# First token's middle row: folded and split once for all batches, kept in DRAM, and put into each transform by DMA

## The chip, the cores and the metric

The kernel runs on one core of a Trainium2 chip. The core has five engines that work side by side and wait for one another through semaphores: TensorE (PE, with its weight loads as PEld), VectorE (DVE), ScalarE (ACT), GpSimd (POOL) and SyncE (SP), which here only issues DMAs. The metric is the device time of one execution in microseconds (us).

## The reference

Inputs are q, k, v of 4 batches, 8 heads, 768 tokens and 64 elements, and two weights. A window attention with four sink tokens gives x, and a Fourier mix with a feed-forward part follows:

```
B, H, S, D = q.shape                                   # 4, 8, 768, 64
scores = scale * matmul(q, k.transpose(0, 1, 3, 2))
keep = is_sink | in_window                             # 4 first keys, or the last 128
a = exp(scores - max); a = a / (sum(a) + 1e-09)
x = matmul(a, v)                                       # then to (B, S, H * D = 512)

X = fft(fft(x, axis=1), axis=2)                        # along tokens, then along the 512 columns
u = x + real(X)
un = (u - mean(u)) / sqrt(var(u) + 1e-06)
out = u + maximum(un @ w_ch1, 0.0) @ w_ch2
```

## The kernel before

**Stages.** The attention runs over 24 query blocks of 128 tokens (6 for each batch), each in four steps of one pair of heads, so 96 steps in all. Then the feed-forward part runs over six groups of four blocks; it takes the rest of the time and is not touched.

**The transform of one batch** is done inside the attention of the next batch, by the function `fourier`. Token n and token 768 - n enter the cosine sum with the same factor and the sine sum with opposite ones, and so do columns m and 512 - m. So the six blocks of a batch are first folded to three: `fold_n` adds and subtracts blocks j and 3 + j (one 128x512 operation on VectorE, one on GpSimd), `fold_m` folds the columns (128x255), `fold_hi` on ScalarE rounds the result to the short float that TensorE takes at speed (`gh`), and `fold_lo` on VectorE keeps the remainder (`gl`). Then come `stage1` (products with the constant matrices, into the banks `za`, `zr`, `zb`) and `stage2a`/`stage2b`, and `combine` and `update` add the real part to `u`.

**The first token** fits no pair: block 3 has a place for it in its row 0, but while the fold runs that place holds token 384 in another role. So the outputs of the first token are worked out apart for all batches at once, in steps 10 to 20 (`first_products` to `first_row`), and kept in DRAM (`x0_dram`, 32 rows of 64). Each transform reads its 512 numbers back (`load_row`, 33 equal copies, into the tile `xr`) and does four small operations with them:

- `put_row` (L379): copies the row into row 0 of block 3 of `u`, once the fold has read that block.
- `mid_sum` (L368): folds its columns, 33x255.
- `mid_hi` (L371): rounds the folded row into rows 0 to 32 of the tile `sph`, 33x257.
- `mid_row` (L376): replaces row 32 of `sph` by the remainder, 1x257.

Rows 0 and 32 of `sph` are what `stage1` uses: its last product into `za` and `zr` takes `sph` and adds the first token. The other rows of `sph` meet zeros. [...] All four operations are on VectorE, but for `mid_hi` of the last batch, which is on ScalarE.

**The order.** Up to step 97 the order of each engine is written out by hand: `at(step, engine, function)` puts a function into a step, and the table `SCHEDULE` says where in the step the events ("A", 0 to 3, "V", "G", "T") stand among the attention's own operations. An event "S" is issued by SyncE at the head of its step, behind the loads of q, k and v that belong there. After step 97 a scheduler sets the order; the fold and transform of the last batch fall into that part, together with the start of the feed-forward part and with the conversion of its weights (`convert`, L600 to L602, tiles `raw`, `cv`, `w2r`, three VectorE operations for each 512 columns).

**Buffers that set the pace.** A pair's scores `s` have two PSUM buffers: TensorE can write the scores of a pair when VectorE has read those of the pair before last (`merge` L727, `soft1` L739 with `sm` and `mx`). A block of v (`ldv`) has four buffers. SyncE issues its DMAs strictly in order, so a DMA that waits holds all behind it.

Of the kernel before, what the change touches and what calls it, by code (L numbers as in the profile page):

```python
# [11 lines left out]
F32 = mybir.dt.float32  # L12
F32R = mybir.dt.float32r
# [3 lines left out]
ALU = mybir.AluOpType  # L17
# [3 lines left out]
B, H, S, D = 4, 8, 768, 64  # L21
DM, DFF = H * D, 2048
# [3 lines left out]
NHALF = NB // 2  # L26
# [8 lines left out]
NR = 33  # L35
# [26 lines left out]
FILL_AT, FILL = (24, 36), 0  # L62
FOLD_AT, FOLD_LAST, FOLD_ENG = (0, 4, 8), (0, 4, 8), "VG"

F_N, F_M, F_S, ROW = (3, 3), (4, 5), (6, 7), (5, 8, 10)
EV_A = 0

SINK0_AT = 3, 3, "V"
# [143 lines left out]
def kernel(  # L212
# [14 lines left out]
    nc = tc.nc  # L227
    V, A, G, T = nc.vector, nc.scalar, nc.gpsimd, nc.tensor

    def f32(ap):  # L230
        return ap.bitcast(F32)
# [3 lines left out]
    dpool = ctx.enter_context(tc.tile_pool(name="dpool", bufs=1, space=bass.MemoryType.DRAM))  # L235
# [3 lines left out]

    w_dram = [dpool.tile([P, 2, len(LEFT) * 2 * P], F32, name=f"w2s{q}") for q in range(NF // 2)]  # L240
    x0_dram = dpool.tile([B * H, D], F32, name="x0d")


    prm = cpool.tile([P, 2, 2], I32, name="prm")
# [22 lines left out]
    def run(general):  # L267
        tag = "g" if general else ""
        with ExitStack() as p1:
# [5 lines left out]
            fw = pf.enter_context(tc.tile_pool(name="fw" + tag, bufs=1))  # L275
            ev = {}

            def at(s, eng, fn):
                ev.setdefault((s, eng), []).append(fn)
# [26 lines left out]
            sph = fpool.tile([P, 384], F32R, name="sph")  # L306
# [3 lines left out]
            def uview(b):  # L310
                if b not in us:
                    us[b] = ([U[b][:, j] for j in range(NB)] if b in U else
                             [fw.tile([P, DM], F32, tag=f"us{j}", name=f"us_{b}_{j}") for j in range(NB)])
                return us[b]
# [5 lines left out]
            def bank(b, name):  # L320
# [5 lines left out]
                pool, t, n = banks[turn[0] % len(banks)]  # L326
                return pool.tile([P, 512], F32, tag=t, name=f"{name}_{b}", bufs=n)

            def fourier(b, at, ready):
                u = uview(b)  # L330
                gh = npool.tile([P, NHALF, DM], F32R, tag="gh", name=f"gh_{b}", bufs=1)
# [3 lines left out]
                t_ = {}  # L335
# [3 lines left out]
                    return t_[name]  # L339

                def load_row():
                    t_["x0"] = fw.tile([NR, DM], F32, tag="xr", name=f"xr_{b}")
                    nc.sync.dma_start(t_["x0"], x0_dram[H * b:H * b + H].rearrange("(o h) d -> o (h d)", o=1).broadcast_to([NR, DM]))

                def fold_n(eng, j, odd):
                    t = fw.tile([P, DM], F32, tag=f"f{odd}", name=f"f{odd}_{b}_{j}", bufs=2 - odd)
# [16 lines left out]
                def fold_lo(j):  # L363
                    V.tensor_tensor(gl[:, j], t_.pop(("g", j)), f32(gh[:, j]), op=ALU.subtract)  # L364

                def mid_sum():
                    r = t_["x0"]
                    V.tensor_tensor(r[:, 1:256], r[:, 1:256], r[:, 511:256:-1], op=ALU.add)  # L368

                def mid_hi():  # L370
                    (A.copy if b == B - 1 else V.tensor_copy)(sph[:NR, :257], t_["x0"][:, :257])  # L371

                def mid_row():
                    t = t_["x0"]
                    lo = sph[NR - 1:NR, :257]
                    V.tensor_tensor(lo, t[NR - 1:NR, :257], f32(lo), op=ALU.subtract)  # L376

                def put_row():
                    V.tensor_copy(u[NHALF][0:1], t_["x0"][0:1])  # L379

                def stage1(kind, mc, part, parts):
                    ps = t_[f"z{kind}{mc}"] if part else psum(f"z{kind}{mc}")
# [77 lines left out]
                        nc.sync.dma_start(u_dram[b][:, blk, :], t)  # L460

                tail = b == B - 1 or general
                at(1, "S", load_row)
                for j in range(NHALF):
                    k = ready[j]
                    e0, e1 = FOLD_TAIL if tail else FOLD_ENG
# [4 lines left out]
                    at(k + F_M[1], e1, lambda j=j: fold_m(eng[e1], j, 1))  # L471
                    at(k + F_S[0], "A", lambda j=j: fold_hi(j))
                    at(k + F_S[1], "V", lambda j=j: fold_lo(j))
                at(ready[0] + ROW[0], "V", put_row)
                at(ready[0] + ROW[1], "V", mid_sum)
                at(ready[0] + ROW[2], "A" if b == B - 1 else "V", mid_hi)
                at(ready[0] + ROW[2], "V", mid_row)
                k = ready[2] + S1
                n1, na, nb = PARTS_TAIL if tail else PARTS[b]
                for i, (kind, mc) in enumerate((("a", 0), ("a", 1), ("r", 0), ("b", 0), ("b", 1))):  # L480
                    n = n1[i]
# [10 lines left out]
                for i, j in enumerate(FFT_ORDER):  # L492
# [9 lines left out]
                    for r in range(2):  # L502
                        e = UPD_TAIL[r] if b >= B - 2 else "G"
                        n = 2 * i + r
# [147 lines left out]
            hp = []  # L652

            def window_attention(fourier, load_constants):
                with ExitStack() as pa:
                    kpool = pa.enter_context(tc.tile_pool(name="kpool", bufs=1, side="right"))
# [187 lines left out]
                    with ExitStack() as man:  # L844
# [6 lines left out]
                        def take(n, rows=P, dtype=F32):  # L851
                            took[0] += n
                            t = scratch[:rows, took[0] - n:took[0]]
                            return t if dtype == F32 else t.bitcast(dtype)
# [66 lines left out]
                        x0 = take(D, B * H)  # L921
# [19 lines left out]
                        def first_row(i):  # L941
                            if i == 0:
                                V.tensor_scalar(fs[:, 0], fs[:, 0], fm[:, 2:3], None, op0=ALU.mult)
                                V.tensor_scalar(x0, fin[:, 1 + NS], fs[:, 0, 0:1], None, op0=ALU.mult)
                            else:
                                V.scalar_tensor_tensor(x0, fin[:, 1 + NS + i], fs[:, 0, i:i + 1], x0, op0=ALU.mult, op1=ALU.add)
                            if i == NS - 1:
                                nc.sync.dma_start(x0_dram, x0)
# [12 lines left out]
                        at(15, "A", first_exp)  # L961
                        for i in range(NS):
                            at(17 + i, "V", lambda i=i: first_row(i))

                        table = {
                            "merge": merge, "soft1": soft1, "expo": expo, "sink_p": sink_p, "trans_p": trans_p, "copy_p": copy_p,
# [4 lines left out]
                        s = 0  # L971
                        extra.append(lambda name: ps_t.tile([P, 512], F32, tag="x", name=name)
                                     if s % NP in X_AT and not X_NOT[0] <= s <= X_NOT[1] and s < len(steps) - 2 else None)
                        while s < last:
# [21 lines left out]
                            if s == 0:  # L996
                                a, b, e = SINK0_AT
                                at(a, "A", lambda: sink_hi(0))
                                at(b, e, lambda: sink_lo(0))
                            for e in "AVGT":  # L1000
                                for op in SCHEDULE[s >= PHASE][e][k]:
                                    if op in EVENTS:
                                        if (s, op) == (4, "G"):
                                            load_constants()
                                        run_ev(s, op)
                                    elif op in STEP_LAG:
                                        lag(table[op], s, STEP_LAG[op])
                                    else:
                                        at_ = s - BLOCK_AT[op]
                                        if at_ % NP == 0 and 0 <= at_ // NP < NQ:  # L1010
                                            table[op](at_ // NP)
                                            if op == "store_x" and at_ // NP % NB == 3:
                                                b = at_ // NP // NB
                                                fourier(b, lambda d, e, f, s=s: at(s + d, e, f), FOLD_AT if b < B - 1 else FOLD_LAST)
                            s += 1
                    extra.clear()
                return last

            def general_attention(fourier):
                for b in range(B):  # L1020
                    u = uview(b)
                    with ExitStack() as pa:
# [19 lines left out]
                        for j, blk in enumerate(Q_BLOCKS):  # L1042
# [22 lines left out]
                            for h in range(H):  # L1065
                                r = slice(D * (h % 2), D * (h % 2) + D)
# [24 lines left out]
                        x0 = gw.tile([1, DM], F32, tag="gq", name=f"gx0_{b}")  # L1091
                        V.tensor_copy(x0, u[NHALF][0:1])
                        V.tensor_copy(u[NHALF][0:1], u[0][0:1])
                        nc.sync.dma_start(x0_dram[H * b:H * b + H].rearrange("(o h) d -> o (h d)", o=1), x0)
                    ev = []
                    fourier(b, lambda d, e, f: ev.append((d, ENGINES.index(e), len(ev), f)), FOLD_AT)
                    for it in sorted(ev, key=lambda t: t[:3]):
                        it[3]()

            if general:  # L1100
                load_constants()
                general_attention(fourier)
                normalize(0, 8, 22, lambda i: None)
                start_ffn(40)
                s = 0
                while ev:
                    for e in ENGINES:
                        run_ev(s, e)
                    s += 1
            else:  # L1110
                s = window_attention(fourier, load_constants)
# [322 lines left out]
            with tc.manual_schedule():  # L1434
# [3 lines left out]
                for g in range(1, len(groups)):  # L1438
# [70 lines left out]
                    for _ in steps:  # L1509
                        pass  # L1510

    run(False)
    with tc.tile_pool(name="tpool2", bufs=1) as tp:
        t0 = tp.tile([P, 2], F32, name="t1")
# [8 lines left out]
    with tc.If(general != 0):  # L1523
        run(True)
# [77 lines left out]
```

## Time and profile before

| | |
|---|---|
| median of 3 runs | 768.49 us (767.43 to 771.24) |
| the profiled execution's own time | 768.74 us |
| its span | 767.0 us |
| TensorE busy | 742.3 us (97%) |
| VectorE busy | 600.6 us (78%) |
| ScalarE busy | 345.9 us (45%) |
| GpSimd busy | 181.6 us (24%) |

How to read the rows in this document. A row of a timeline has start, duration, engine, line, operation, output and inputs, and in brackets how long the engine had been idle and what released it. A row of the chain of waits has start, duration on the chain, engine, output tile and line; the chain is followed back from the last instruction, at each step to what released it. A row of the windows has the stretch in us, then busy time (and instructions) of TensorE, its weight loads, VectorE, ScalarE and GpSimd, then the granted TensorE clock (1.00 is full), the share of the DMA engines and GB/s. Matmul ends are modelled.

The attention and the four transforms take the first 283 us of the span. The folds of the four batches stand at about 48 to 72 us, 100 to 130 us, 158 to 190 us and 215 to 235 us.

### The profile page before, as it was taken

The numbers are of one execution on the slowest core, as the hardware profiler recorded it, in microseconds if no ns is written. First come the engines' busy times: TensorE is split into PE (matmuls) and PEld (weight loads), VectorE is DVE, ScalarE is ACT, GpSimd is POOL, SyncE is SP. The second block draws the span as 40 slices with busy tenths as digits, with TensorE's granted clock in tenths as the row PEclk, the third lists the DMA queues.
The fourth block names the chain that finished last, engine by engine and source line by source line (L and its number), as shares of the span: only waits on it lengthen the run. The fifth ranks groups of instructions, "written<-read, shape, count | busy, mean of one in ns | idle before, by whom it ended". The sixth has DMA issues, their size and how long they took to land.

```text
span 767.0 us, 14157 instructions
## 1 busy us (share of the span) xinstructions
PE 742.3 (97%) x4903; PEld 626.7 (82%) x4903; DVE 600.6 (78%) x1641; ACT 345.9 (45%) x896; POOL 181.6 (24%) x286
## 2 busy tenths in 40 slices
PE   7999998998999999999999999999999999999996
PEld 5666775766788778788989899899899998998995
DVE  6878588799799989969877978778895888764435
ACT  4877666666643223444545333333333333333330
POOL 2557267467574445400000000000000000000001
PEclk9999999999999999999999999999999999999998
DMA  9845514532313446323546757755577557556661
GB/s 294 277 112 165 144 56 151 160 104 94 111 56 138 138 165 219 110 110 141 190 151 247 227 160 231 230 171 191 170 226 235 173 172 243 160 176 188 208 193 60
DMA packets 95008, 129.40 MB, mean 169 GB/s; under 512 B 5932, under 2 KB 60844, under 8 KB 94544
## 3 DMA queue, kind: packets, MB, share of 16 engines
q1 hardware_dynamic: 94352, 124.26, 51.1%
q0 software_dynamic: 288, 3.76, 1.3%
q8 instruction: 41, 0.67, 0.4%
q10 hardware_dynamic: 288, 0.39, 0.1%
q14 instruction: 39, 0.32, 0.1%
HBM read 104.26 MB, written 24.13 MB: 167 GB/s over the span
## 4 chain that ended last, share of the span: by engine, by line
PE 78%; DVE 16%; issue 2%; ACT 1%; POOL 1%; DMA 1%; SPq 0%; DVEq 0%; ACTq 0%; POOLq 0%
PE h L638 31%; PE p L1313 25%; PE xt L808 5%; PE s L721 5%; PE o L1139 3%; PE pt L770 2%; PE za L393 2%; PE zb L393 1%; DVE f L348 1%; PE x L820 1%; DVE sm L739 1%; DVE gl L364 1%; PE zr L393 1%; DVE w2r L602 1%; DMA vt<-in_v_sink_dram 1%
## 5 line engine op out<-in xcount | busy, mean ns | idle before, releaser
L1313 PE MATMUL p<-w_ring,h_sums 128*128 128x256 f32 x936 | 131.3, 283 | 0.1
L1313 PEld LDWEIGHTS p<-w_ring,h_sums 128*128 128x128 f32 x936 | 122.9, 191 | 3.6 <-DVE u L1143 0.3
L1261 ACT CAST h_sums<-sums 128x256 fp32r<-128x256 f32 (+2 forms) x158 | 89.7, 568 | 70.5 <-PE p L1313 28.6
L1262 DVE TENSOR_TENSOR h_sums<-sums,h_sums 128x256 fp32r<-128x256 f32 (+2 forms) x158 | 98.3, 622 | 17.5 <-ACT h_sums L1261 16.5
L1313 PE MATMUL p<-w2t,h_sums 128*128 128x256 f32 x702 | 110.3, 283 | 0.0
L1335 POOL TENSOR_TENSOR u<-u,u 128x512 f32<-128x512 f32 x3 | 3.8, 1293 | 422.9 <-DVE u L1335 422.9
L1313 PEld LDWEIGHTS p<-w2t,h_sums 128*128 128x128 f32 x702 | 97.9, 191 | 3.1
L638 PE MATMUL h<-un_slots,w 128*128 128x512 f32 x396 | 96.5, 392 | 0.0
L638 PE MATMUL h<-un_last,w 128*128 128x512 f32 x396 | 96.4, 392 | 0.0
L638 PEld LDWEIGHTS h<-un_slots,w 128*128 128x128 f32 x396 | 72.7, 188 | 14.0
L638 PEld LDWEIGHTS h<-un_last,w 128*128 128x128 f32 x396 | 72.3, 188 | 14.4 <-DVE un_slots L553 0.7
L745 ACT ACTIVATE sm<-sm,mx 128x132 f32<-128x132 f32 x192 | 75.8, 399 | 14.4 <-DVE mx L739 14.4
L1475 ACT ACTIVATE sums<-h 128x512 f32<-128x512 f32 x40 | 23.9, 597 | 96.8 <-PE h L638 96.8
L721 PE MATMUL s<-ring,q 64*128 64x260 f32 x320 | 55.6, 430 | 7.2 <-DVE mx L739 7.2
L1163 DVE STREAM_TRANSPOSE unf<-un 32x128 f32<-32x128 f32 x192 | 58.1, 302 | 2.8
L1272 DVE TENSOR_TENSOR sums<-sums 128x256 f32<-128x256 f32 x39 | 16.4, 422 | 47.6 <-ACT sums L1475 47.3
L1443 ACT ACTIVATE sums<-h 128x512 f32<-128x512 f32 x40 | 23.9, 599 | 64.8 <-PE h L638 64.8
L739 DVE CUSTOM_DVE_ANT_0 sm<-s,mask 128x132 f32<-128x132 f32 x192 | 47.5, 285 | 4.5 <-PE s L719 2.4
L727 DVE COPY_PREDICATED s<-older,s 128x256 f32<-128x256 uint8 x80 | 33.8, 422 | 16.9 <-PE s L721 16.6
L721 PEld LDWEIGHTS s<-ring,q 64*128 64x128 f32 x320 | 25.0, 186 | 21.3 <-issue 10.0
L808 PE MATMUL xt<-ptl,ldv 128*64 128x128 f32 x384 | 39.8, 288 | 0.0
L745 ACT ACTIVATION_READ_ACCUMULATOR sm<-sm,mx 128x1 f32 x192 | 36.7, 191 | 0.0
(239 smaller groups left out, 1378.1 us busy)
## 6 DMA issues: line engine op xcount, KB each, us to landing
w_ring<-w2s SPq DMA_DIRECT2D x62, 512.0 KB, 4.3
w2t<-w2s SPq DMA_DIRECT2D x93, 256.0 KB, 3.2
raw<-in_moe_w_ch_dram SPq DMA_DIRECT2D x32, 512.0 KB, 3.3
w2s<-w_ring SPq DMA_DIRECT2D x16, 512.0 KB, 3.0
ldv<-in_v_dram SPq DMA_DIRECT2D x28, 256.0 KB, 2.8
ring<-in_qk_dram SPq DMA_DIRECT2D x24, 264.0 KB, 4.3
w2s<-w2t SPq DMA_DIRECT2D x24, 256.0 KB, 3.1
out_dram<-u SPq DMA_DIRECT2D x22, 256.0 KB, 4.6
```

What stands on the lines that cost most here:

```text
L393: T.matmul(ps[:, :NK], a, c, start=i == 0, stop=i == len(mm) - 1)
L638: T.matmul(ps[:, :tb], a[:, cs], x[:, :, cc, :], start=n == 0, stop=n == 3 * NCC - 1)
L721: T.matmul(ps[:, j, :P + W], st["q", g][rows, hp, :], keys(g, 2 * hp + j), start=True, stop=True)
L727: V.copy_predicated(ps[:, :, P + NS:P + W], older[qi > 2], ps[:, :, 0:P])
L739: V.tensor_tensor_reduce(sm[:, h % 4], ps[:, j, P:P + W], mask[min(qi, 3)], -SCALE, 3.0e38, ALU.add, ALU.min, accum_out=mx[:, 0, h:h + 1])
L745: A.activation(sm[:, h % 4], sm[:, h % 4], AF.Exp, bias=mx[:, 0, h:h + 1], scale=-1.0, accum_out=mx[:, 1, h:h + 1])
L808: T.matmul(ps[D * j:D * j + D, p, :], st["v", kb(g) - i][:, h, :], a[:, h % 4, :], start=i == 0, stop=i == n - 1)
L1163: V.transpose(unf[32 * q:32 * q + 32, :, r], un[r].rearrange("p (c q j) -> p c q j", c=NCC, q=4)[:, :, q])
L1261: A.copy(hc_hi[:, left(a, n)], src)
L1262: V.tensor_tensor(hc_lo[:, left(a, n)], src, f32(hc_hi[:, left(a, n)]), op=ALU.subtract)
L1313: T.matmul(acc[i][:, 2 * P * tp:2 * P * tp + 2 * P], x, w, start=q == 0 and tp == 0 and n == 0, stop=q == end and n == 2, skip_group_check ...
L1443: A.activation(r4[:, 0].rearrange("p t w -> p (t w)"), ps, AF.Relu)
```

## The change

The four operations on the row leave the transforms. A new function `middle_rows` does the fold and the split once for all four batches, in four partitions (one per batch), in steps 24 to 29 of the attention, and stores both halves in DRAM (`xm_dram`, per batch two rows of 257). Each transform then issues two DMAs on SyncE: `load_row` brings the two half rows straight into rows 0 and 32 of `sph`, nine steps after the start of `fourier`, and `put_row` brings the 512 numbers from `x0_dram` straight into row 0 of block 3, five steps after it.

```diff
-F_N, F_M, F_S, ROW = (3, 3), (4, 5), (6, 7), (5, 8, 10)
+F_N, F_M, F_S, ROW = (3, 3), (4, 5), (6, 7), (9, 5)
+ROW_AT = 24, 26, 27, 28, 29
...
+    xm_dram = dpool.tile([B, 2, DM // 2 + 1], F32, name="xmd")
...
+            def middle_rows(b, n, at):
+
+                x = fw.tile([B, DM], F32, tag="xr", name=f"xr_{b}")
+                xm = fw.tile([B, 2, DM // 2 + 1], F32R, tag="xm", name=f"xm_{b}")
+
+                def load():
+                    nc.sync.dma_start(x[:n], x0_dram[H * b:H * (b + n)].rearrange("(o h) d -> o (h d)", o=n))
+
+                def fold():
+                    V.tensor_tensor(x[:n, 1:256], x[:n, 1:256], x[:n, 511:256:-1], op=ALU.add)
+
+                def hi():
+                    A.copy(xm[:n, 0], x[:n, :257])
+
+                def lo():
+                    V.tensor_tensor(xm[:n, 1], x[:n, :257], f32(xm[:n, 0]), op=ALU.subtract)
+
+                def store():
+                    nc.sync.dma_start(xm_dram[b:b + n], f32(xm[:n]))
+
+                for s, e, fn in zip(ROW_AT, "SVAVS", (load, fold, hi, lo, store)):
+                    at(s, e, fn)
+
...
                 def load_row():
-                    t_["x0"] = fw.tile([NR, DM], F32, tag="xr", name=f"xr_{b}")
-                    nc.sync.dma_start(t_["x0"], x0_dram[H * b:H * b + H].rearrange("(o h) d -> o (h d)", o=1).broadcast_to([NR, DM]))
+                    nc.sync.dma_start(f32(sph[:NR:NR - 1, :257]), xm_dram[b])
...
-                def mid_sum():
-                    r = t_["x0"]
-                    V.tensor_tensor(r[:, 1:256], r[:, 1:256], r[:, 511:256:-1], op=ALU.add)
-
-                def mid_hi():
-                    (A.copy if b == B - 1 else V.tensor_copy)(sph[:NR, :257], t_["x0"][:, :257])
-
-                def mid_row():
-                    t = t_["x0"]
-                    lo = sph[NR - 1:NR, :257]
-                    V.tensor_tensor(lo, t[NR - 1:NR, :257], f32(lo), op=ALU.subtract)
-
                 def put_row():
-                    V.tensor_copy(u[NHALF][0:1], t_["x0"][0:1])
+                    nc.sync.dma_start(u[NHALF][0:1], x0_dram[H * b:H * b + H].rearrange("(o h) d -> o (h d)", o=1))
...
-                at(1, "S", load_row)
+                at(ROW[0], "S", load_row)
...
-                at(ready[0] + ROW[0], "V", put_row)
-                at(ready[0] + ROW[1], "V", mid_sum)
-                at(ready[0] + ROW[2], "A" if b == B - 1 else "V", mid_hi)
-                at(ready[0] + ROW[2], "V", mid_row)
+                at(ready[0] + ROW[1], "S", put_row)
...
+                        middle_rows(0, B, at)
```

In the order of VectorE, the second fold of batch 1 reads before (the tiles `sm` and `mx` are softmax rows of a pair, `s_2` and `s_3` the scores of the block's third and fourth pair, `older` a mask):

```order
L739 ISA sm_2_1766,mx_1707<-s_2_1722,mask_133 128x132
L739 ISA mx_1707 128x1
L371 CAST sph<-xr_1449 33x257
L376 TENSOR_TENSOR sph<-xr_1449,sph 1x257
L727 COPY_PREDICATED s_3_1750<-older_129,s_3_1750 128x2x128
L739 ISA sm_2_1766,mx_1707<-s_3_1750,mask_133 128x132
```

And the same place now:

```order
L748 ISA sm_2_1768,mx_1708<-s_2_1724,mask_134 128x132
L748 ISA mx_1708 128x1
L736 COPY_PREDICATED s_3_1752<-older_130,s_3_1752 128x2x128
L748 ISA sm_2_1768,mx_1708<-s_3_1752,mask_134 128x132
L748 ISA mx_1708 128x1
```

The rounding of the row and its remainder have gone from between the softmax of the third and the fourth pair; nothing has come in their place. Batches 0 and 2 read the same.

In the order of SyncE, the stretch around the fold of batch 0 reads before (`q`, `ring` and `ldv` are the loads of queries, keys and values for blocks further on):

```order
L686 DMA ring<-in_k_mid_dram 128x4x132
L343 DMA xr_770<-x0d 33x512
L690 DMA ldv_796<-in_v_dram 128x512
L690 DMA ldv_894<-in_v_dram 128x512
L681 DMA q_899<-in_qk_dram 128x4x128
L683 DMA ring<-in_qk_dram 128x4x132
```

And the same place now:

```order
L337 DMA xr_172<-x0d 4x512
L695 DMA ring<-in_k_mid_dram 128x4x132
L699 DMA ldv_799<-in_v_dram 128x512
L349 DMA xmd<-xm_173 4x514
L391 DMA u_64<-x0d 1x512
L699 DMA ldv_900<-in_v_dram 128x512
L690 DMA q_905<-in_qk_dram 128x4x128
L692 DMA ring<-in_qk_dram 128x4x132
L690 DMA q_926<-in_qk_dram 128x4x128
L692 DMA ring<-in_qk_dram 128x4x132
L367 DMA sph<-xmd 2x257
```

The store of the split rows and the row for `u` (L391) now stand ahead of one load of v and of the next queries and keys; the load of `sph` (L367) stands four loads later.

In the scheduled part, VectorE reads before at the first fold of batch 3:

```order
L348 TENSOR_TENSOR f_3_0_3076<-us_0_2618,us_3_2621 128x512
L358 TENSOR_TENSOR f_3_0_3074<-f_3_0_3074 128x255
L379 COPY us_3_2621<-xr_3030 1x512
L355 TENSOR_TENSOR f_3_0_3074<-f_3_0_3076 128x255
L368 TENSOR_TENSOR xr_3030<-xr_3030 33x255
L602 SCALAR_TENSOR_TENSOR cv_3176<-raw_3069,cv_3176 128x512
L836 TENSOR_TENSOR us_4_2622<-x_3093,mx_2749 128x512
L364 TENSOR_TENSOR gl_3019<-f_3_0_3074,gh_3018 128x512
```

And now:

```order
L372 TENSOR_TENSOR f_3_0_3070<-us_0_2614,us_3_2617 128x512
L382 TENSOR_TENSOR f_3_0_3068<-f_3_0_3068 128x255
L611 SCALAR_TENSOR_TENSOR cv_3170<-raw_3063,cv_3170 128x512
L379 TENSOR_TENSOR f_3_0_3068<-f_3_0_3070 128x255
L609 TENSOR_SCALAR cv_3267<-raw_3107 128x512
L610 SCALAR_TENSOR_TENSOR cv_3267<-raw_3107,cv_3267 128x512
L845 TENSOR_TENSOR us_4_2618<-x_3087,mx_2745 128x512
L388 TENSOR_TENSOR gl_3015<-f_3_0_3068,gh_3014 128x512
```

The copy and the fold of the row are gone, and the scheduler has moved two operations of the next weight conversion (`cv_3267`) up to their place; they stood behind the last fold before.

More of the change, by code (lines that the diff above doesn't have):

```diff
@@ L1095, in general_attention @@
                     ev = []
+                    middle_rows(b, 1, lambda s, e, fn: fn())
                     fourier(b, lambda d, e, f: ev.append((d, ENGINES.index(e), len(ev), f)), FOLD_AT)
```

## The prediction

> **What bounds the kernel now.** I read the page first, for the span and the chain of waits:
>
> ```profile
> span 767.0 us, 14157 instructions
> PE 78%; DVE 16%; issue 2%; ACT 1%; POOL 1%; DMA 1%; SPq 0%; DVEq 0%; ACTq 0%; POOLq 0%
> ```
>
> TensorE carries most of the chain, so a VectorE operation that goes is worth something only where VectorE is on the chain. Next I asked for the instructions on the tile that the change removes, `xr` (count, then shortest/median/longest in ns):
>
> ```profile
> L368 DVE TENSOR_TENSOR xr<-xr x4: 404/436/1486, 58.4 to 219.2; 33x255 f32<-33x255 f32 x4
> L376 DVE TENSOR_TENSOR sph<-xr,sph x4: 418/735/777, 63.1 to 225.6; 1x257 fp32r<-1x257 f32 x4
> L371 DVE CAST sph<-xr x3: 282/757/1408, 62.8 to 176.5; 33x257 fp32r<-33x257 f32 x3
> L379 DVE COPY us<-xr x2: 846/868/889, 105.5 to 218.1; 1x512 f32<-1x512 f32 x2
> ```
>
> The first three cost 0.28 to 0.42 us at their shortest and up to 1.49 us where they meet other work; 33 partitions or one make no difference. Then I followed the chain through the four folds. These pieces of it are removed:
>
> ```profile
> 58.49 1.41 DVE xr L368
> ...
> 113.69 0.33 DVE xr L368
> ...
> 117.82 0.69 DVE sph L371
> ...
> 118.53 0.74 DVE sph L376
> ...
> 171.09 0.39 DVE xr L368
> ...
> 176.63 1.34 DVE sph L371
> ...
> 177.99 0.73 DVE sph L376
> ...
> 218.14 0.77 DVE us L379
> ...
> 219.17 0.40 DVE xr L368
> ...
> 225.64 0.78 DVE sph L376
> ```
>
> `put_row` of batches 0 to 2 and the two later operations of batch 0 are not on it. A removed piece is worth at most the wait of TensorE behind it, so the last view is TensorE's own idle time, in brackets at the row's end:
>
> ```profile
> 60.48 0.71 PE L721 MATMUL s<-ring,q 64*128 64x260 f32 x4 [0.94 <-DVE mx L739]
> 61.11 0.42 PEld L808 LDWEIGHTS xt<-ptl,ldv 128*64 128x64 f32 x8 [0.34 <-POOL ptl L786]
> ...
> 123.95 1.24 PE L721 MATMUL s<-ring,q 64*128 64x260 f32 x4 [2.40 <-DVE mx L739]
> ...
> 172.05 0.71 PE L721 MATMUL s<-ring,q 64*128 64x260 f32 x4 [0.87 <-DVE mx L739]
> ...
> 180.39 0.66 PE L820 MATMUL x<-ident,xs 128*128 128x128 f32 x4 [1.03 <-DVE un_slots L553]
> ...
> 183.58 0.71 PE L721 MATMUL s<-ring,q 64*128 64x260 f32 x4 [0.74 <-DVE mx L739]
> ```
>
> In each fold TensorE's scores wait until the softmax on VectorE has emptied a bank, since the fold stands in VectorE's queue between them.
>
> **The change part by part.** The sum is made against the profiled execution's own 768.7 us (its span of 767.0 and 1.7 around it), which is the 768.5 of the median within 0.3.
>
> *Batch 0.* TensorE waited 0.94, and 1.41 goes ahead of it. But 0.6 us later its products `xt` wait for GpSimd (`ptl`, second row above), which the removed operation does not hold. So nearly all is caught there: between 0 and 0.94, and I take 0.3, near the lower end, because that row stands so close behind.
>
> *Batch 1.* 0.33 + 0.69 + 0.74, with 0.05 between them, is 1.8 of an unbroken VectorE chain that ends in the wait of 2.40. Taken alone the three cost 0.33 + 0.28 + 0.42 = 1.0, if what delayed them delays their successor instead. Between 1.0 and 1.8; I take 1.7, because the successors are a merge and a softmax that read PSUM, and these hold to their means over the whole attention (busy us, mean ns of one | idle before):
>
> ```profile
> L739 DVE CUSTOM_DVE_ANT_0 sm<-s,mask 128x132 f32<-128x132 f32 x192 | 47.5, 285 | 4.5 <-PE s L719 2.4
> L727 DVE COPY_PREDICATED s<-older,s 128x256 f32<-128x256 uint8 x80 | 33.8, 422 | 16.9 <-PE s L721 16.6
> ```
>
> `put_row` (up to 0.89) gives nothing in these three batches: it is not on the chain.
>
> Behind this wait stands a second cost. Two windows of 4 us and the chain show it; the last two rows are the same work some 4 us later:
>
> ```profile
> 120.00:124.00 4.00, 1.60 (x14) 0.98 (x12) 4.00 (x13) 1.68 (x7) 4.00 (x5) 0.98 0.57 152
> 124.00:128.00 4.00, 4.00 (x26) 2.83 (x28) 2.31 (x13) 2.24 (x10) 3.77 (x9) 0.59 0.00 0
> ```
>
> ```profile
> 123.95 1.24 PE s L721 x4
> 125.19 1.90 PE xt L808 x16
> ...
> 128.78 0.64 PE s L721 x4
> 129.42 1.02 PE xt L808 x16
> ```
>
> The granted clock was 0.59 in the 4 us after the wait: 1.24 + 1.90 where 0.64 + 1.02 would do, 1.5 lost. After waits of 0.94 and 1.03 no such stretch follows. With 1.7 gone the wait falls to 0.7, so the loss should go: between 0 and 1.5, I take 1.4. [...]
>
> *Batch 2.* 0.39 + 1.34 + 0.73, with 0.05 between, is 2.5 of the chain; TensorE waited 0.87 + 1.03 + 0.74 = 2.64 behind it. The first part meets only the first wait (0.39 of 0.87), the rest the other two (1.77). At most 2.2; alone the three cost 0.33 + 0.28 + 0.42 = 1.0. I take 2.0, near the upper end, because VectorE has no idle time between the removed pair and the last wait.
>
> *Batch 3* lies in the scheduled part, where VectorE also converts weights and is never idle, and ScalarE's rounding goes as well:
>
> ```profile
> 220.00:240.00 20.00, 19.38 (x109) 16.51 (x105) 19.94 (x38) 8.00 (x17) 8.98 (x7) 1.00 0.23 79
> ```
>
> 0.77 + 0.40 + 0.78 = 1.95 goes. TensorE is nearly full too; what it waits for VectorE from 209 to 283 us is 1.4 + 0.5 + 0.4 = 2.3 (us in total, times, longest):
>
> ```profile
> PE a L420 <- DVE zb L408: 1.4, 1, 1.4
> PE za L393 <- DVE d L447: 0.5, 1, 0.5
> PE o L1139 <- DVE h L1132: 0.4, 1, 0.4
> ```
>
> At most 1.9. The scheduler also moved two conversion operations ahead of a block's output; at worst that gives back most of it, so between 0.5 and 1.9; I take 1.7.
>
> *What is added.* Two VectorE operations in four partitions (about 0.4 each by the `xr` rows) and one on ScalarE, just ahead of batch 0's fold. No VectorE piece stands on the chain there, so between 0 and 0.8 lost; I take 0.1.
>
> *The new DMAs.* `put_row` on SyncE waits until the fold has read block 3, and holds the load of a v block and the next queries and keys:
>
> ```profile
> 50.80 1.46 POOL L348 TENSOR_TENSOR f<-u 128x512 f32<-128x512 f32 x1
> ...
> 41.59 6.37 SPq L690 DMA_DIRECT2D ldv<-in_v_dram x2
> ...
> 64.43 0.44 PE L808 MATMUL xt<-ptl,ldv 128*64 128x128 f32 x4
> ```
>
> ```profile
> ldv<-in_v_dram SPq DMA_DIRECT2D x28, 256.0 KB, 2.8
> ```
>
> GpSimd ends its fold at 52.3, the held load was issued by 48.0, so it comes 4.3 us later, lands by 52.3 + 0.4 + 2.8 = 55.5 and is first used at 64.43: nearly 9 us of cover. The load of `sph` follows four loads later, and its first user starts at 75.9 us:
>
> ```profile
> L393 PEld LDWEIGHTS za<-cst_row,sph x8: 187/188/190, 75.9 to 235.7; 128*128 128x128 f32 x8
> ```
>
> So I cost them at nothing, from 0 to a small loss that only the last rival prices. The removed 33-fold row loads gave SyncE one issue per batch; it issues six more in all now, and of the 6.37 us that it took for two loads in the row above nearly all was waiting.
>
> **The sum:** 0.3 + 1.7 + 1.4 + 2.0 + 1.7 - 0.1 = 7.0, so 768.7 - 7.0 = 761.7 us. What comes after the folds is bound by TensorE, so a shift there carries to the end. With all lower ends (0, 1.0, 0, 1.0, 0.5, less 0.8) 1.7 is left, 767.0; with all upper ends (0.94, 1.8, 1.5, 2.2, 1.9) 8.3, 760.4.
>
> **The rivals.**
>
> 1. *GpSimd or ScalarE takes the place of VectorE.* For: in batch 1 GpSimd is busy 4.00 and 3.77 of 4 us in the two windows above, and its product for the second next `xt` ends only at 125.7:
>
> ```profile
> 125.10 0.63 POOL L794 TENSOR_SCALAR_AFFINE_SELECT pta<-pta 128x512 f32<-128x512 f32 x1
> ```
>
> The user of that stands at 129.42, and 3.2 us less puts it at 126.2, so it just holds; against, then. If it fails, as in batch 0, nothing is left of batch 0 and half of the other four terms: 0.85 + 0.7 + 1.0 + 0.85 = 3.4, less 0.1, so 765.4. Chance 0.19.
>
> 2. *The scheduled part turns out worse.* Conversion ahead of the fold delays `gl` of batch 3, and TensorE's `za` waits for it: batch 3 gives -1.5 instead of 1.7, so 764.9. Chance 0.07.
>
> 3. *The slow stretch has another cause than the wait and stays.* For: waits of 0.94 and 1.03 show none, so where it begins is not known; against: it starts with the first product after the wait. Without its 1.4 the gain is 5.6, so 763.1. [...] Chance 0.09.
>
> 4. *Slower: SyncE stands too long at `put_row`.* Its place is the wait for the fold in batches 0 to 2, its price one us of TensorE for each us beyond the cover. It decides once the row is issued later than 64.4 - 3.2 = 61.2 us, nearly 9 us after the fold's end; three times 5 us beyond that would give 768.7 + 15 - 7.0 = 776.7. Nothing in the rows points to it. Chance 0.05.
>
> That the change leaves the operations in place is ruled out by the order of VectorE, where they are missing.
>
> **How the numbers follow.** The forecast has 0.60, rival 3 0.09, rival 1 0.19, rival 2 0.07, rival 4 0.05. Half a per cent, which is about what a measurement of this kernel can tell from no change, is 3.8 us. Faster by more than that are the forecast and rival 3, and a little of rivals 1 and 2 on their near side: 0.72. Within it is the rest of those two: 0.23. Slower: 0.05. The range runs from 759.2, a little under the sum of the upper ends for waits of GpSimd's that shorten too, to 767.8, a little over the sum of the lower ends.
>
> **What would show it.** In the changed kernel's profile: no wait of TensorE near 2.4 us in batch 1's fold and a granted clock near 1.00 in all windows of 4 us there; TensorE's waits on VectorE in batch 2's fold under 0.7 in all; those from 209 to 283 us under 0.6; VectorE's busy time lower by about 4 x 0.44 + 4 x 0.74 + 3 x 0.76 + 2 x 0.87 - 2 x 0.4 = 7.9 us by the medians above. Wrong it would be if waits on `ptl`, `pta` or `sk` of GpSimd had grown by what VectorE's shrank, if another window showed a clock under 0.9, or if the first `xt` after a `put_row` waited for a DMA.

## The result, and the profile after

The changed kernel takes 762.82 us (median of 7, 761.46 to 764.46) beside 768.49 before; the ratio is 0.9925, with a 95% interval of 0.9907 to 0.9942. That is 5.7 us less, where 7.0 was forecast. Its profiled execution took 764.07 us, 4.7 less than that of before. Its page:

```profile
span 762.3 us, 14152 instructions
PE 739.3 (97%) x4903; PEld 625.4 (82%) x4903; DVE 596.1 (78%) x1628; ACT 345.9 (45%) x896; POOL 179.8 (24%) x286
```

VectorE is busy 4.5 us less, not 7.9. To see where the time came from, one product that each of the 24 query blocks has (`x` from `vs` and `skt`) serves as a mark. In the kernel before, the marks of blocks 3, 5, 7, 12, 13, 19 and 22 (counted from 0) start at

```profile
45.43 0.48 PE L822 MATMUL x<-vs,skt 128*128 128x512 f32 x1
58.42 0.48 PE L822 MATMUL x<-vs,skt 128*128 128x512 f32 x1
74.19 0.48 PE L822 MATMUL x<-vs,skt 128*128 128x512 f32 x1
120.44 0.48 PE L822 MATMUL x<-vs,skt 128*128 128x512 f32 x1
132.11 0.48 PE L822 MATMUL x<-vs,skt 128*128 128x512 f32 x1
190.68 0.48 PE L822 MATMUL x<-vs,skt 128*128 128x512 f32 x1
218.51 0.48 PE L822 MATMUL x<-vs,skt 128*128 128x512 f32 x1
```

and in the changed one at

```profile
45.01 0.48 PE L831 MATMUL x<-vs,skt 128*128 128x512 f32 x1
58.49 0.48 PE L831 MATMUL x<-vs,skt 128*128 128x512 f32 x1
73.11 0.48 PE L831 MATMUL x<-vs,skt 128*128 128x512 f32 x1
119.36 0.48 PE L831 MATMUL x<-vs,skt 128*128 128x512 f32 x1
128.21 0.48 PE L831 MATMUL x<-vs,skt 128*128 128x512 f32 x1
184.51 0.48 PE L831 MATMUL x<-vs,skt 128*128 128x512 f32 x1
212.34 0.48 PE L831 MATMUL x<-vs,skt 128*128 128x512 f32 x1
```

The difference of two rows is the gain up to there; how much it grows from one mark to the next is the gain of that stretch, and the last stretch ends with the span. The first 0.42 is not counted to the change: it varies from -2.6 to +0.7 over the profiles below, most of all because some executions run a few us near 16 us at a lower clock (in four of the 14 profiles a window of 4 us there has 0.50 to 0.77).

| stretch | forecast | blocks | gain |
|---|---|---|---|
| added operations | -0.1 | 3 to 5 | -0.49 |
| batch 0's fold | +0.3 | 5 to 7 | +1.15 |
| batch 1's fold and the clock behind it | +1.7 + 1.4 | 12 to 13 | +2.82 |
| batch 2's fold | +2.0 | 13 to 19 | +2.27 |
| batch 3, scheduled part | +1.7 | 22 to the end | -1.47 |

With the 0.42 these make 4.7. The three folds gave what was forecast or more; the added operations cost more, and batch 3 went the other way. In batch 1 the two windows now read

```profile
120.00:124.00 4.00, 2.99 (x30) 1.94 (x30) 3.80 (x18) 2.81 (x14) 3.85 (x8) 1.00 0.28 77
124.00:128.00 4.00, 3.81 (x36) 2.82 (x35) 1.94 (x8) 2.89 (x11) 3.85 (x8) 1.00 0.93 274
```

The clock is full in both. TensorE's waits on VectorE from 100 to 130 us (us in total, times, longest) shrank from one of 2.4 to

```profile
PE s L730 <- DVE mx L748: 1.0, 1, 1.0
```

and its waits on VectorE in batch 2's fold (158 to 190 us) from 2.64 in all to

```profile
PE s L730 <- DVE mx L748: 0.7, 2, 0.5
```

In the scheduled part, from 205 to 285 us, they are

```profile
PE a L432 <- DVE zb L420: 1.6, 1, 1.6
PE za L405 <- ACT asb L441: 1.2, 1, 1.2
PE h L647 <- POOL w_gl L636: 0.6, 1, 0.6
PE b L453 <- DVE d L459: 0.6, 1, 0.6
PE za L405 <- DVE d L459: 0.5, 1, 0.5
```

4.5 us, where the same stretch of the kernel before has the three rows of the prediction (2.3) and 0.6 for `w_gl`, 2.9. The waits for `asb` and for `d` ahead of `b` are new.

SyncE did what was forecast. It issues `put_row` when GpSimd's fold has ended (at 52.44), the held load of v right behind it (the forecast had 52.7), and the load of `sph` 5 us later:

```profile
52.47 0.24 SPq L391 DMA_DIRECT2D u<-x0d  x1
52.80 0.36 SPq L699 DMA_DIRECT2D ldv<-in_v_dram  x1
...
57.65 0.56 SPq L367 DMA_DIRECT2D sph<-xmd  x1
```

TensorE waits for none of them.

### The profile page after: what moved, and what is told of

It reads as the page before. It is cut to its first block, busy times and chain, and to the rows that moved or that the text cites. A ratio compares the mean times of both kernels' runs of the same rounds, so it can differ in the third digit from the quotient of the medians.

```text
span 762.3 us, 14152 instructions
## 1 busy us (share of the span) xinstructions
PE 739.3 (97%) x4903; PEld 625.4 (82%) x4903; DVE 596.1 (78%) x1628; ACT 345.9 (45%) x896; POOL 179.8 (24%) x286
## 4 chain that ended last, share of the span: by engine, by line
```

## The experiments

**What was open.** Why batch 3 gave nothing, and whether the clock behind batch 1's wait is truly the wait's doing. For batch 3, theory A says that the new order which the scheduler formed without the four operations costs more than they did. Theory B is the forecast: they are worth 1.7, and what is missing went elsewhere. Theory C says that the stretch neither gains nor loses. Each of the other tests names its own theories. Diffs are against the changed kernel, medians are of 5 or 6 executions (12 for two kernels), and "b3" is the gain from block 22 to the end by the marks.

b3 also takes in the feed-forward part, which is not touched. A finer mark is TensorE's last `b` product, which ends the transforms. It starts in the kernel before and in the changed one at

```profile
272.91 0.96 PE L441 MATMUL b<-cst,zb 128*128 128x258 f32 x6
267.86 0.95 PE L453 MATMUL b<-cst,zb 128*128 128x258 f32 x6
```

so 54.40 and 55.52 us after block 22: -1.12. The gain from block 22 to this mark is called b3t. Profiles with one order agree in it within 0.1, but for the toss told below; from this mark to the end they differ by up to 0.6.

**The changed kernel again.**

> The changed kernel once more, beside the three that follow. Both theories: 762.8 us, 5.7 below the kernel before (between 4.0 and 7.1 by the interval of the first measurement). In the profile the gain at the attention's block marks should stand at about 6.5 us when the last fold begins (222 us) and fall to about 4.7 by 235 us, with TensorE waits of about 0.6 (b on VectorE's d) and 1.2 (za on ScalarE's asb) between 215 and 230 us.

762.72 us, ratio 0.9914 (0.9888 to 0.9940). The other stretches repeat to 0.1, but b3 is +0.16, not -1.47, and b3t +0.46, not -1.12: the fall to 4.7 that was expected did not come. The waits from 205 to 285 us are

```profile
PE za L405 <- ACT asb L441: 1.2, 1, 1.2
PE a L432 <- DVE zb L420: 0.8, 1, 0.8
PE b L453 <- DVE d L459: 0.6, 1, 0.6
PE h L647 <- POOL w_gl L636: 0.6, 1, 0.6
```

So 1.6 of the loss of the first profile comes in some executions and not in others (more on it below); the two new waits stay.

**Batch 3 in the old way.**

```diff
+ROW_OLD = 5, 8, 10
+SPLIT, PUT = (0, 1, 2), (0, 1, 2)
...
-                at(ROW[0], "S", load_row)
+                if not (b in SPLIT and b in PUT):
+                    at(1, "S", load_x0)
+                if b in SPLIT:
+                    at(ROW[0], "S", load_row)
...
-                at(ready[0] + ROW[1], "S", put_row)
+                if b in PUT:
+                    at(ready[0] + ROW[1], "S", put_row)
+                else:
+                    at(ready[0] + ROW_OLD[0], "V", put_row)
+                if b not in SPLIT:
+                    at(ready[0] + ROW_OLD[1], "V", mid_sum)
+                    at(ready[0] + ROW_OLD[2], "A" if b == B - 1 else "V", mid_hi)
+                    at(ready[0] + ROW_OLD[2], "V", mid_row)
```

`load_x0` loads the row 33-fold, and `put_row` of a batch that is not in `PUT` copies it, both as the kernel before did. The next kernels set other batches in the two lists.

> Batch 3 in the old way (row loaded 33-fold, four small operations on VectorE and ScalarE), batches 0 to 2 by DMA. The scheduled part then has the order of the kernel before. Theory A (the change's new order of the scheduled part costs more than the removed operations give): faster than the changed kernel by 1.3 to 1.8, so 761.0 to 761.5, and no TensorE wait for ScalarE's asb in batch 3's first products. Theory B (my forecast: the four operations are worth 1.7 there, and what is missing went elsewhere): slower than the changed kernel by 1.7, 764.5. Theory C (the part gains and loses nothing; the difference of the two profiles there is chance): 762.8.

763.15 us, ratio 0.9923 (0.9896 to 0.9949); b3 -0.30, b3t +0.01. The time is nearest to theory C; its interval takes in A and B too. The wait for `asb` is gone, as A had it, and the waits of before are back, 2.9 in all. A's figure had been sized on the unlucky profile: beside the better one of the changed kernel (+0.46) the old operations in the old order lose 0.45, beside the worse one they gain 1.1. The operations and the order are the kernel before's here, so the -0.30 of b3 is what chance does behind the transforms.

**Batch 3 alone by DMA.**

```diff
+SPLIT, PUT = (3,), (3,)
```

> Only batch 3 by DMA, batches 0 to 2 in the old way; the scheduled part has the order of the changed kernel. Theory A: 0.5 lost on the added operations and 1.5 in the scheduled part, so 2.0 above the kernel before, 770.5. Theory B: 0.1 lost and 1.7 gained, so 766.9. Theory C: 0.5 lost, 769.0.

768.73 us, ratio 0.9995 (0.9978 to 1.0012); b3 +0.34, b3t +0.44, the added operations -0.57. The time is nearest to C again. Its profile holds one more thing: batch 1 is in the old way here, TensorE waits its 2.4 there, and yet that stretch gained 1.39, for the clock stayed full:

```profile
PE s L762 <- DVE mx L780: 2.4, 1, 2.4
```

```profile
120.00:124.00 4.00, 1.78 (x13) 1.13 (x12) 3.98 (x13) 1.43 (x6) 4.00 (x5) 1.00 0.61 167
124.00:128.00 4.00, 3.60 (x33) 2.35 (x33) 3.33 (x19) 3.45 (x13) 3.77 (x10) 1.00 0.24 54
```

This parts the 2.82 of batch 1: 1.39 is the clock, 1.43 the shorter wait. Of this kernel's 12 executions, 8 have a mean clock under 0.997, which the test of batch 1 below takes as the sign of a slow stretch.

**Batch 3 with only the row for u by DMA;** `mid_sum`, `mid_hi` and `mid_row` of batch 3 are back on their engines, but, as it turned out, not in their old places.

```diff
+SPLIT, PUT = (0, 1, 2), (0, 1, 2, 3)
```

> Batch 3's row for u by DMA, but its fold, rounding and remainder in the old way (two operations on VectorE, one on ScalarE); batches 0 to 2 by DMA. TensorE keeps the changed kernel's order, VectorE too but for the two operations that stand between. Theory A (order): not faster than the changed kernel, 762.8 to 764.0, and 1.3 or more slower than the kernel with batch 3 in the old way, although it has one operation less than that. Theory B: between the two, 763.8. Theory C: 762.8, all three alike.

763.22 us, ratio 0.9918 (0.9893 to 0.9943); b3 -0.12, b3t +0.45. The three operations cost next to nothing, but they do not stand in batch 3's fold (209 to 226 us here). The scheduler ran them far ahead of it:

```profile
53.19 0.41 DVE L378 TENSOR_TENSOR xr<-xr 33x255 f32<-33x255 f32 x1
199.06 0.39 ACT L381 CAST sph<-xr 33x257 fp32r<-33x257 f32 x1
200.12 0.42 DVE L386 TENSOR_TENSOR sph<-xr,sph 1x257 fp32r<-1x257 f32 x1
```

From block 22 on VectorE and ScalarE run the changed kernel's order, and b3t is its +0.46 again. So this test says nothing on what the operations would cost inside the fold in the new order. It does show that they can stand where they cost at most 0.1 by the marks.

**Batch 1 in the old way.**

```diff
+SPLIT, PUT = (0, 2, 3), (0, 2, 3)
```

> Batch 1 alone in the old way (its row loaded 33-fold, four operations on VectorE), the other three by DMA. Theory A (the three operations on the chain lengthen TensorE's wait in batch 1's fold to about 2.4, and a wait of that length brings the stretch at half clock behind it): 2.8 above the changed kernel, 765.5, most executions with a granted clock of 0.995 and a 4-us window near 0.59 behind the wait; those at 0.997 or 0.998 about 1.4 faster than those. Theory B (the stretch comes by chance, whatever the wait): 1.4 above, 764.1, executions at 0.995 no commoner than in the changed kernel (2 of 13 so far).

766.88 us, ratio 0.9973 (0.9956 to 0.9991), 4.1 above the changed kernel, more than either theory wrote. The stretch of batch 1 gives back its 2.8 (+0.03). The profile's b3 is -1.89 (b3t -1.46), of the unlucky kind and 0.4 beyond the changed kernel's; how many of the other executions are so is not known, so 1.3 of the 4.1 stays open. The wait and the slow clock are back:

```profile
123.39 1.24 PE L762 MATMUL s<-ring,q 64*128 64x260 f32 x4 [2.43 <-DVE mx L780]
```

```profile
120.00:124.00 4.00, 1.57 (x10) 0.84 (x9) 4.00 (x10) 1.93 (x9) 3.92 (x7) 0.87 0.40 106
124.00:128.00 4.00, 3.87 (x29) 2.43 (x25) 1.95 (x13) 2.26 (x8) 3.68 (x8) 0.70 0.08 12
```

In the kernel before, the same work took 1.24 + 1.90 us in the slow stretch and 0.64 + 1.02 some 4 us later, 1.9 times as long; taking the slow clock as half, 0.13 + 0.30 of 4 us is by estimate 3.4 us of it. The mean clock of an execution shows whether it had such a stretch, here or near 16 us (0.992 to 0.996 in the six profiles with one, 0.997 to 0.999 in the eight without): 8 of this kernel's 12 are under 0.997, as are the 8 of 12 with batch 3 alone by DMA, against 3 of 19 of the changed kernel. So the slow stretch comes with the wait (theory A), but not every time: of the 45 executions of the kernel before that ran beside these kernels, 8 are at 0.997 and over. Their median span is 765.4 us, and 766.85 for the 24 at 0.994 to 0.996: 1.45 apart, beside the 1.4 of the forecast.

**The added operations on GpSimd.**

```diff
-                    V.tensor_tensor(x[:n, 1:256], x[:n, 1:256], x[:n, 511:256:-1], op=ALU.add)
+                    G.tensor_tensor(x[:n, 1:256], x[:n, 1:256], x[:n, 511:256:-1], op=ALU.add)
...
-                for s, e, fn in zip(ROW_AT, "SVAVS", (load, fold, hi, lo, store)):
+                for s, e, fn in zip(ROW_AT, "SGAGS", (load, fold, hi, lo, store)):
```

> The two added VectorE operations (fold and remainder of the four rows) on GpSimd. Theory A (the added fold holds the softmax, TensorE waits 0.64 for mx behind it, and that is the 0.4 to 0.5 lost ahead of batch 0's fold): 0.4 faster than the changed kernel, 762.3, the block marks losing nothing between block 3 and block 4. Theory B (GpSimd is late for the next ptl, or stretches VectorE's operations): same or up to 0.5 slower, 762.7 to 763.2.

763.98 us, ratio 0.9936 (0.9913 to 0.9960): slower, as in theory B, and 0.8 beyond what B wrote. The wait of 0.6 for `mx` ahead of batch 0's fold (its row stands further below) is gone, as A had it, and from 45 to 56 us there is this one instead:

```profile
PE pk L835 <- ACT pta L786: 0.5, 1, 0.5
```

From block 3 to block 7 this profile gains 0.86, the changed kernel's 0.66 to 0.86. So the move gained nothing, and it lost nothing there either. Why the kernel is slower is not shown: the profile lost 1.2 ahead of block 3 (its mean clock is 0.996, beside 0.997 in the changed kernel's), and some 0.3 lies outside the span in its six executions (1.93 to 2.11 us there, at most 1.85 in any other kernel).

**The order of before without the four operations.** Order edges alone hold about 60 VectorE and 23 ScalarE instructions, and one product of TensorE, to their old succession:

```diff
+                for e, seq in WANT.items():
+                    for (t0, k0), (t1, k1) in zip(seq, seq[1:]):
+                        i, j = made[e, t0, k0], made[e, t1, k1]
+                        tc.add_manual_dep(j.ins, i.ins.name, mybir.DependencyInfo(mybir.DependencyClass.NoSync, mybir.DependencyReason.DATA), reason="order")
```

> The changed kernel, but in the fold of batch 3 VectorE, ScalarE and TensorE are held to the order of the kernel before without the four removed operations (by order edges only; about 60 VectorE and 23 ScalarE instructions and one product of TensorE). Theory A (the removed operations are worth 1.7 there and the scheduler's new order ate it): 761.0 to 762.2, no wait for ScalarE's asb, sum of TensorE's waits from 205 to 285 us under 2.0. Theory C (freed VectorE time is worth nothing there, whatever the order): 762.7, waits of 2.8 to 3.3 in sum as in the four kernels so far.

761.71 us, ratio 0.9906 (0.9881 to 0.9930); b3 +0.83, b3t +1.20. The time is A's, though its interval reaches C's 762.7; the marks part them. The waits are close to what A had, 2.0 in all and none for `asb` (instructions of these engines all carry the recorder's line here):

```profile
PE b L243 <- DVE d L243: 0.8, 1, 0.8
PE h L243 <- POOL w_gl L658: 0.6, 1, 0.6
PE o L243 <- DVE h L243: 0.4, 1, 0.4
PE za L243 <- DVE d L243: 0.2, 1, 0.2
```

By b3t, beside the order of before with the operations (+0.01) they are worth 1.2; beside their absence in the new order (+0.46), the order is worth 0.7. The order is not quite that of before: `gh` of the first fold stands one place earlier on ScalarE, one `za` product earlier on TensorE, and from 241 us on, behind the held stretch, a few neighbours on VectorE and GpSimd have changed places. What these give is not parted from the 1.2.

**Only the half rows by DMA**, the row for `u` copied on VectorE in all batches.

```diff
+SPLIT, PUT = (0, 1, 2, 3), ()
```

> The half rows by DMA in all batches, but the row for u copied on VectorE as before (from a row loaded 33-fold). By my forecast the copy is worth nothing in batches 0 to 2 and 0.77 in batch 3: 763.5. Rival (it is worth nothing in batch 3 either): 762.7. Second rival (it delays a softmax in batches 0 to 2 by its 0.3 to 0.9): 763.6 to 764.5.

761.02 us, ratio 0.9895 (0.9872 to 0.9919): below all that was written. Batches 0 to 2 stay as they were (+1.19, +2.77, +2.27), so the copy is worth nothing there, as forecast; b3 is +1.60, b3t +1.84. With the copy in its queue the scheduler had formed a third order.

**The same beside the changed kernel, and the copy in batch 3 alone.** The kernel that copies in all batches (once more) and the one that copies in batch 3 alone have one order on TensorE and ScalarE, and but for three copies on VectorE; the second differs from the changed kernel in batch 3 only. Its lists:

```diff
+SPLIT, PUT = (0, 1, 2, 3), (0, 1, 2)
```

> The changed kernel a third time, beside the next three. 762.7 by both theories.

> Half rows by DMA, row for u copied on VectorE, once more. Theory A (its scheduled part has a better order, with TensorE's waits of 205 to 285 us at 1.7 in sum where the changed kernel has 3.3 to 4.6): 1.0 to 1.7 faster than the changed kernel beside it, 761.0 to 761.7. Rival (the difference between the two earlier calls was chance): 762.7.

> The changed kernel with one edit: in batch 3 alone the row for u is copied on VectorE, one operation more on the busiest engine of that stretch. The scheduled part then has the order of the kernel that copies it in all batches. Theory A (the order decides there): as that kernel, 761.0 to 761.7, 1.0 or more faster than the changed kernel although it does more. Rival 1 (that kernel gained in batches 0 to 2, where SyncE issues no DMA for the row): 762.7, as the changed kernel. Rival 2 (my forecast: the copy costs its 0.77): 763.5.

762.68, 761.09 and 761.61 us, ratios 0.9922 (0.9905 to 0.9940), 0.9899 (0.9883 to 0.9916) and 0.9907 (0.9891 to 0.9923); b3 -1.38, +1.76 and +1.46, b3t -1.06, +1.86 and +1.81. The intervals overlap, so the times alone do not part the last from the first; the marks do. One operation more on the busiest engine (VectorE, 19.94 of 20 us from 220 to 240 us in the kernel before) made batch 3 1.3 us faster than in the better of the changed kernel's profiles, by b3 and b3t alike. That the copy also takes a DMA out of SyncE's queue is not the reason by the waits: from 205 to 285 us no engine waits for a DMA in either profile. With the copy, TensorE's waits from 205 to 285 us are

```profile
PE za L427 <- ACT asb L463: 0.8, 1, 0.8
PE h L679 <- POOL w_gl L668: 0.6, 1, 0.6
PE b L475 <- DVE d L481: 0.3, 1, 0.3
```

**The toss.** Two of the changed kernel's three profiles have the worse b3. Up to one instruction VectorE runs alike in both kinds; these are VectorE and GpSimd at that place in the one with +0.16

```profile
226.93 1.90 POOL L636 TENSOR_TENSOR w<-cv,w 128x512 fp32r<-128x512 f32 x1 [3.81 <-issue]
227.00 0.68 DVE L610 SCALAR_TENSOR_TENSOR w2r<-raw,w2r 128x512 int32<-128x512 int32 x1
```

and in the one with -1.38:

```profile
225.90 1.28 POOL L636 TENSOR_TENSOR w<-cv,w 128x512 fp32r<-128x512 f32 x1 [3.80 <-issue]
225.98 1.76 DVE L610 SCALAR_TENSOR_TENSOR w2r<-raw,w2r 128x512 int32<-128x512 int32 x1
```

They begin within 0.08 us of each other, GpSimd's first in both. Either GpSimd's operation is longer by 0.62, or VectorE's by 1.08, and VectorE's delay goes on to `d` and `zb`, which TensorE waits for: the extra 0.5 and 0.8 of its waits. What lengthens the one or the other is not shown here, and the starts, GpSimd's ahead by 0.07 to 0.08 in both kinds, do not tell which it will be. In the seven profiles with this order at that place, it fell three times on VectorE; in the four with the third order, where the pair stands side by side too, never.

**The added operations earlier**, in the kernel that copies the row on VectorE.

```diff
-ROW_AT = 24, 26, 27, 28, 29
+ROW_AT = 22, 23, 24, 25, 26
```

> The kernel that copies the row in all batches, with the added operations two or three steps earlier (22 to 26 in place of 24 to 29). Theory A (the added fold costs 0.4 to 0.5 because it stands ahead of a softmax that TensorE waits 0.64 for, and elsewhere it need not): 0.4 faster than its neighbour, 760.6 to 761.2, no loss between block 3 and block 5. Rival (every place in VectorE's queue there costs the same): as its neighbour.

760.67 us, ratio 0.9891 (0.9875 to 0.9907); the loss from block 3 to block 5 is 0.10, where its neighbour has 0.56. Theory A by the marks; the interval takes in the neighbour's time. By block 7, behind batch 0's fold, 0.3 of the difference is left. In the changed kernel the added fold takes 0.73 and stands ahead of the softmax that TensorE waits for:

```profile
47.18 0.73 DVE L340 TENSOR_TENSOR xr<-xr 4x255 f32<-4x255 f32 x1
```

```profile
48.40 0.50 PE L728 MATMUL s<-ld 64*128 64x132 f32 x4 [0.64 <-DVE mx L748]
```

Two steps earlier it takes 0.41 and no wait for `mx` follows. This is the fastest kernel here, 8.2 below the median of before that ran beside it (768.84), against 6.2 for the changed kernel.

## Why the prediction was nearly right, and which term was wrong

- **Bound and mechanism.** That TensorE waits in each fold for VectorE's softmax, and that the row's operations are on that chain, holds for batches 0 to 2: the waits shrank (from 0.94, 2.40 and 2.64 to none, 1.0 and 0.7), and the gain stayed to the end. That the sum of 7.0 came within 1.3 of the measured 5.7 is in part luck: batch 0 gave 0.9 more than its term, which made up for part of what batch 3 did not give.
- **Batch 1 (1.7) and the clock (1.4):** 1.43 and 1.39. Rival 3, by which the slow stretch stays, fell in this kernel. The lower clock followed the wait of 2.4 in most executions and not in all: a mean clock under 0.997 stands in 8 of 12 with batch 1 in the old way and in 37 of 45 of the kernel before. What decides it, no run here shows.
- **Batch 2 (2.0):** 2.27, just above its upper end of 2.2. The waits give 1.9 of it; the rest was not taken apart.
- **Batch 0 (0.3, at most 0.94):** 1.15 to 1.25. The row for `ptl`, which was to catch nearly all, was misread: it is a row of the weight loads (PEld), and no product (PE) waited there. Some 40 rows of `xt` weight loads have this 0.34 ahead of them, in both kernels. It stands at the same place now, and a wait for `pta` that follows has grown:

```profile
59.98 0.42 PEld L817 LDWEIGHTS xt<-ptl,ldv 128*64 128x64 f32 x8 [0.34 <-POOL sk L765]
62.76 0.25 PE L835 MATMUL pk<-ident_r,sk 128*128 128x128 f32 x1 [0.89 <-ACT pta L786]
```

  In the profile of the changed kernel run again, the 0.94 is gone and with it 0.28 more: the eight products around it, 0.71 for each four when the wait parted them, take 1.15 in one run. The wait for `pta` grew from 0.61 to 0.89 and took 0.28 back. Some 4 us later, `xt` products on `pta` follow those on `ptl` 0.27 sooner. Together that is 1.2.
- **Added operations (0.1):** 0.39 to 0.49 by three profiles. "No VectorE piece stands on the chain there" was true of the kernel before; the added fold is what put one there.
- **SyncE (nothing):** right; `put_row` issued at 52.47 and the load behind it at 52.80. Rivals 1 and 4 did not happen: waits on `ptl` and `pta` grew by no more than the 0.28 above, and no product waited for a DMA.
- **Batch 3 (1.7, at least 0.5): the step that failed.** It gave +0.16 or -1.4 by b3, +0.46 or -1.1 by b3t, by execution. The step took 1.95 of VectorE's rows out of 2.3 of TensorE's waits and let the moved conversion operations take back all but 0.5 at worst. What happened is rival 2's place with another wait: in the new order TensorE stands 0.6 for `d` and 1.2 for `asb`, which ScalarE empties only behind `gh`, a cast and a `relu` (0.62, 0.62 and 0.59 in the profile of the changed kernel run again), and the wait for `zb` shrank from 1.4 to no less than 0.8. So its waits on VectorE, which were to fall under 0.6 there, are 1.4 or 2.7. Without the operations and nearly in the order of before, b3t is 1.2; the new order takes 0.7 of that back, and the toss 1.5 more where it falls on VectorE. The term should have been a range that takes in zero, because the order of that part is not the programmer's.
- **VectorE's busy time** fell by 4.5 or, in the better profile, 6.2, and not by 7.9, although the sum of 7.9 had left out two more copies of 0.41. The operations that remain take longer: those of the weight conversion (`cv`, `w2r`) 1.5 to 3 us in all.

What stays open: why the scheduler's third order, with the copy, is better by 0.6 in b3t than the order of before without it. It was found by chance. One piece shows in the waits: TensorE's 0.4 for `h`, which the order of before has with and without the operations, is gone. Beside the new order, one conversion operation that stood within batch 3's fold runs 8.7 us later, the second `f` and `gh` come earlier, and the last `zb` has moved ahead of a conversion operation; no run takes these apart.

## What to carry to other kernels

Where a scheduler sets the order, an operation's price is not what it takes but what the next order is like: price such a stretch with a range around zero, and compare a few orders before keeping one. A small operation that is added once, ahead of a wait that is zero so far, can cost most of its length (here 0.4 to 0.5 of 0.73); try it a few steps to either side. Split a gain by marks that every execution has: the 4.7 of one profile hid +6.2 in three folds and 2.0 lost in two places. And look up where a scheduler has put the operations of a test before reading its time.

## What the hardware showed that was not expected

- A wait of TensorE of 2.4 us was followed by a lower clock in the profiles of two kernels (0.98 and 0.59, 0.87 and 0.70 in the windows of 4 us from 120 to 128 us; by estimate 3.4 us at half) and by none in that of a third (1.00 and 1.00). At most 37 of 45 executions of the kernel before had such a stretch, counted by a mean clock under 0.997; some of these may have lost it near the start. In the changed kernel's profile the wait of 1.0 was not followed by one (1.00 and 1.00). Each of the 14 profiles also has one wait for VectorE of 1.48 to 2.56 us that ends near 14 us. Behind the seven under 2.1 the clock stayed full (1.00); four of the seven from 2.15 on were followed by a window of 4 us at 0.50 to 0.77. With batch 1's three that makes six of ten waits from 2.15 to 2.56.
- Two operations that start within 0.08 us of each other on VectorE and GpSimd cost 0.62 on the one or 1.08 on the other, by execution, and 1.5 us at the end of the kernel.
